# Head sums between scores and values, one block for all loops, a shorter VectorE program and partial sums to row 11, in a decode attention kernel

## Chip, cores, metric

The kernel runs on one core of one Trainium2 chip. The metric is the device time of one execution in microseconds (us), the median of several. The spans in the profile lines are one to three us shorter than the time.

## The reference

One token for each of two sequences: a layer norm, attention over a cache of 32,768 keys and values per head (32 query heads share 8 key/value heads), an output projection, and a small gated MLP whose result multiplies the attention.

```python
q = (xn @ wq) ...                                   # [2, 32, 1, 128]
scores = einsum("bhqd,bhkd->bhqk", q, k) * Dh**-0.5
o = einsum("bhqk,bhkd->bhqd", softmax(scores), v)
s = o.reshape(B, Sq, Hq * Dh) @ wo
g = silu(B_ref(xn, w1, w2, w3, w4))                 # the MLP; with one token, w1 and w2 drop out
return x + s * g
```

A pair of sequence and key/value head is a *group*: 16 groups, each with 8.39 MB of keys and 8.39 MB of values, every byte used once. All in all 280.5 MB are read.

## The kernel before

The synchronising engine (SP) issues the loads. Keys have a ring of three half-buffers, values one buffer of a whole group, so a value load must wait until the group before has used its values.

```python
for m in range(1, NG):
    sp.wait_ge(p_k, NPART * m - 1)      # half of the last keys used
    load_k(m)
    sp.wait_ge(s_r, m + 1)              # head sums of the last group done
    load_v(m)
# ... then the output weights wo, in seven pieces:
WO_PARTS = [(0, 0, 8), (0, 8, 16), (1, 0, 8), (1, 8, 12), (1, 12, 14), (1, 14, 15), (1, 15, 16)]
```

VectorE, once per group (cut):

```python
def heads(dst, p0):
    take(dve, s_o)                                   # value products done
    then(dve.tensor_tensor(out=ox, in0=o, in1=sel_t, op=ALU.mult))
    dve.tensor_reduce(out=ob[:, 0:Dh], in_=ox, op=ALU.add).then_inc(s_ob, 1)
    take(dve, s_x)                                   # TensorE has summed over partitions
    then(dve.reciprocal(...)); then(dve.scalar_tensor_tensor(...))
    dve.tensor_reduce(out=dst, in_=xm, ...).then_inc(s_r, 1)

with dve.Fori(0, NG // 2) as t:
    for odd in range(2):
        heads(oA[...], 0)      # head sums of the group before (a dummy in the first)
        group(odd)             # 16 key transposes, then 2 probability transposes
```

TensorE alternates head sums, 64 score products and 64 value products. At the end it multiplies the heads with the output weights: `early` sums all rows of the first half and rows 0 to 11 of the second as wide partial products, which ScalarE copies out and a small product folds in; the last rows go through `product`, four narrow products per row.

```python
early(0); early(1)
pe.wait_ge(s_r, NG + 2)                # last head sums
early(2)
k_e = P(early(3))                      # rows 8 to 11
k_es = A(act.copy(out=e_sb, in_=e_ps))
product(4)                             # rows 12, 13
wait(pe, k_es)
...                                    # fold e_sb into s_ps
for i in range(5, len(WO_PARTS)): mm = product(i)
```

The softmax here doesn't subtract the row's maximum and nothing guards it: scores larger than these inputs give would overflow.

Of the kernel before, what the change touches and what calls it, by code (L numbers as in the profile page):

```python
# [7 lines left out]
F32 = mybir.dt.float32  # L8
# [7 lines left out]
RT = 16  # L16
# [5 lines left out]
WO_PARTS = [(0, 0, 8), (0, 8, 16), (1, 0, 8), (1, 8, 12), (1, 12, 14), (1, 14, 15), (1, 15, 16)]  # L22
# [38 lines left out]
def kernel(  # L61
# [83 lines left out]
    xf, xn = (Ts[0].bitcast(F32)[0:32, i * D:(i + 1) * D] for i in range(2))  # L145
# [25 lines left out]
    def halves(m):  # L171
# [18 lines left out]
    s_t, s_tf, s_z, s_sc, s_e, s_p, s_o, s_ob, s_x, s_on, s_d, s_r, p_k, s_zf, s_tl = (  # L190
        nc.alloc_semaphore(n)
        for n in ("s_t", "s_tf", "s_z", "s_sc", "s_e", "s_p", "s_o", "s_ob", "s_x", "s_on", "s_d", "s_r", "p_k",
                  "s_zf", "s_tl")
# [77 lines left out]
    wait(dve, k_x)  # L271
    k_xf = V(dve.tensor_copy(out=xf, in_=x_bf[0:32, :]))

# [19 lines left out]
    k_xn = layernorm(0, xn, xf, k_xf)  # L293
# [64 lines left out]
    def spread(eng, j, n):  # L358
        return eng.tensor_copy(  # L359
            out=qr[32 * j:32 * j + 32, :, :, :].rearrange("p a e (m n h) -> p (a e) m n h", n=NQ, h=rep)[  # L360
                :, :, :, n, :
            ],
            in_=qT[32 * n:32 * n + 32, 0:B, :].rearrange("p b (t h a) -> p a (b t) h", t=NQB, h=rep),
        )

    wait(pool, k_qT, (g_, g_.n))
    for n in range(NQ):
        for j in range(NQ):
            G(spread(pool, j, n))
# [16 lines left out]
    for n in range(NQ):  # L386
# [20 lines left out]
    k = V(  # L407
        dve.tensor_scalar(
            out=th[:, :, :], in0=th[:, :, :], scalar1=0.5, scalar2=0.5, op0=ALU.mult, op1=ALU.add
        )  # L410
    )
    wait(dve, k)
    k_hb = V(dve.tensor_mul(out=h_bf[:, :, 0:BW:BS], in0=hf, in1=th[:, :, :]))
# [9 lines left out]
    k_tf = V(dve.tensor_add(out=t_f, in0=xn, in1=h2[0:32, :]))  # L423
# [11 lines left out]
    for m in range(1, NG):  # L435
        sp.wait_ge(p_k, NPART * m - 1)
        load_k(m)
        sp.wait_ge(s_r, m + 1)
# [7 lines left out]
    with act.Fori(0, NG):  # L446
        for i in range(NPART):
# [7 lines left out]
            ).then_inc(s_e, 1)  # L455


    zw = z[:, :, :, (NR - 1) * rep:].rearrange("p n e (j w) -> p (n e) j w", j=NQ)[:, :, :, 0:rep]
    wait(pool, (g_, g_.n), (v_, v_.n), (a_, a_.n))
    pool.sem_inc(s_zf, 1)  # L460
    with pool.Fori(0, NG) as m:
# [16 lines left out]
    def group(odd):  # L478
        hs = halves(odd)
        for i in range(NPART):  # L480
            u = odd + hs[i]
            kt = kbuf[:, u * SLOT:(u + 1) * SLOT].bitcast(I32)
            take(dve, s_k[i], 16)
            for r in range(NR):
                take(dve, s_tl if r == T_BUFS - 1 else s_tf)
                dve.transpose(  # L486
                    out=Ts[(NR * i + r) % T_BUFS][:, :].rearrange("p (b t k) -> p t b k", b=NB, t=RT),
                    in_=kt[:, r * W:(r + 1) * W].rearrange("p (t b k) -> p t b k", b=NB, t=RT),
                ).then_inc(s_t, 1)
        for i in range(NPART):  # L490
            h = hs[i]
            take(dve, s_e)
            dve.transpose(  # L493
                out=pts[h][:, :, :].rearrange("p r (t h) -> p t r h", h=rep),
                in_=eps_[i][:, :].rearrange("p (t r h) -> p t r h", r=NR, h=rep),
            )
        dve.tensor_tensor(out=ob[:, Dh:], in0=rss[0][:, :], in1=rss[1][:, :], op=ALU.add).then_inc(s_p, 1)

    def heads(dst, p0):
        take(dve, s_o)  # L500
# [22 lines left out]
    wait(dve, (v_, v_.n), (g_, g_.n), k_x4)  # L523
    dve.sem_inc(s_o, 1)
    dve.sem_inc(s_tf, T_BUFS - 1)
    dve.sem_inc(s_tl, 1)
    with dve.Fori(0, NG // 2) as t:
        for odd in range(2):
            heads(oA[:, bass.ds(t * (2 * RS) + odd * RS, RS)], 0)
            group(odd)  # L530
# [8 lines left out]


    def head_sums():
        take(pe, s_ob)
        mm = pe.matmul(  # L543
            oT, lhsT=sel_h[:, :, :, :].rearrange("p j h w -> p (j h w)"), rhs=ob[:, :], start=True, stop=True
        )
        mm.then_inc(s_x, 1)

    turn = pe.alloc_register("turn")
    pe.reg_mov(turn, 0)
    nc.br("turn", engines=[pe.engine])  # L550
    nc.switch_bb("turn")
    loop = nc.cur_bb
    head_sums()
    pe.reg_add(turn, turn, 1)
    pe.br_lt(turn, NG + 1, on_true="group", on_false="tail")
    nc.switch_bb("group")
    take(pe, s_z)
    with pe.Fori(0, NPART) as i:
        for r in range(NR):
            Tb = Ts[r % T_BUFS][:, :].bitcast(BF16)  # L560
            Tb = Tb.rearrange("p (b c e) -> p b c e", b=NB, e=2)
            zc = (NR - 1 - r) * rep
            take(pe, s_t)
            for nb in range(NB):
                for e in range(2):
                    mm = pe.matmul(  # L566
                        sc2[:, bass.ds(i * 512, 512)], lhsT=z[:, nb, e, zc:zc + 128], rhs=Tb[:, nb, :, e],
                        start=(r == 0 and nb == 0 and e == 0),
                        stop=(r == NR - 1 and nb == NB - 1 and e == 1),
                    )  # L570
            mm.then_inc(s_tf if r < NR - 1 else s_sc, 1)
    take(pe, s_p)
    for h in range(NPART):
        take(pe, s_v[h], 16)
        vt = vbuf[:, h * SLOT:(h + 1) * SLOT].rearrange("p (t d) -> p t d", d=Dh)
        for u in range(NU):
# [111 lines left out]
```

## Time and profile before

| | before |
|---|---|
| time, first three runs | 653.71 us (653.62 to 654.18) |
| busy share TensorE, VectorE | 58%, 58% |
| share of 16 DMA engines' span in data packets | 99.5% |
| bytes read | 280.5 MB |

Busy shares tell how long an engine works, not whether it sets the end. The queue table of the page tells more here: 99.5% of what all DMA engines have is taken. The chain that ended last covers only the last 7.4 us, from the last head sums on, and says nothing of the 645 us before.

### The profile page before, as it was taken

Reading aid. Unit: us, or ns where it says so; the run is one execution under the profiler, and the core shown is the slowest. Engines: PE = TensorE matmul, PEld = TensorE weight load, DVE = VectorE, ACT = ScalarE, POOL = GpSimd, SP = SyncE. Lnnn points to the kernel's source line nnn. Section 1 sums busy time; section 2 is a strip of 40 time slices with the busy share of each in tenths; the row PEclk is TensorE's granted clock in tenths of the full one; section 3 lists DMA queues with packets and bytes.
Section 4 is the critical chain, followed back from the end, with each engine's and each line's share of the span. In section 5 each row is a group of like instructions: output and inputs, shape, how many; then the busy total and the mean of one; then the engine's idle time right before and its main releaser. Section 6 shows DMA issues by size and latency. Waiting matters only on the chain. (4 is left out here: it accounts for less than half of the span.)

```text
span 652.4 us, 6348 instructions
## 1 busy us (share of the span) xinstructions
PE 376.6 (58%) x2164; PEld 140.1 (21%) x2196; DVE 375.5 (58%) x430; ACT 49.4 (8%) x92; POOL 11.9 (2%) x45
## 2 busy tenths in 40 slices
PE   0758392673829458283854819376381946728674
PEld 0213131221213122021321203122130312203221
DVE  6368392754729365481945639285472927548671
ACT  1011010000101001010100101000010100101010
POOL 1200000000000000000000000000000000000000
PEclk9859688785978968597786969769596886959797
DMA  9989998999899989998999899989998999899997
GB/s 387 482 386 450 450 450 386 450 450 450 386 450 450 446 390 450 450 450 386 450 450 450 386 450 450 450 386 450 450 450 386 450 450 450 386 450 420 447 420 322
DMA packets 6509, 280.51 MB, mean 430 GB/s; under 512 B 746, under 2 KB 1004, under 8 KB 1260
## 3 DMA queue, kind: packets, MB, share of 16 engines
q1 hardware_dynamic: 6492, 280.50, 99.5%
q14 instruction: 1, 0.01, 0.0%
q10 hardware_dynamic: 16, 0.00, 0.0%
HBM read 280.50 MB, written 0.00 MB: 430 GB/s over the span
## 5 line engine op out<-in xcount | busy, mean ns | idle before, releaser
L566 PE MATMUL ps<-T,zeros 128*128 128x512 bf16 x992 | 276.5, 425 | 173.2 <-PEq L46 164.4
L486 DVE STREAM_TRANSPOSE T<-kbuf 128x1024 int32<-128x1024 int32 x256 | 291.2, 1207 | 116.5 <-DVEq L46 115.7
L566 PEld LDWEIGHTS ps<-T,zeros 128*128 128x128 bf16 x1024 | 98.8, 104 | 346.1 <-issue 267.8
L579 PE MATMUL ps<-vbuf,pt 128*16 128x512 bf16 x1024 | 71.3, 441 | 40.5 <-PEq L46 40.5
L502 DVE TENSOR_TENSOR ox<-ps,sel_t 128x512 f32<-128x512 f32 x17 | 11.8, 692 | 83.4 <-DVEq L46 83.4
L453 ACT ACT_TABLE_LOAD x16 | 20.5, 1283 | 445.5 <-ACTq L46 445.5
L579 PEld LDWEIGHTS ps<-vbuf,pt 128*16 128x16 bf16 x1024 | 29.8, 101 | 82.1 <-issue 65.2
L493 DVE STREAM_TRANSPOSE pt<-ep 128x512 bf16<-128x512 bf16 x32 | 22.1, 692 | 28.7 <-DVEq L46 28.7
L543 PE MATMUL ps<-ob,sel_h 128*128 128x129 f32 x34 | 9.0, 350 | 39.3 <-PEq L46 39.3
L453 ACT ACTIVATE ep<-ps 128x512 bf16<-128x512 f32 x32 | 19.1, 597 | 104.7 <-ACTq L46 104.5
L507 DVE TENSOR_REDUCE ob<-ox 128x128 f32<-128x512 f32 x17 | 17.3, 1018 | 2.5
L543 PEld LDWEIGHTS ps<-ob,sel_h 128*128 128x128 f32 x34 | 5.8, 212 | 47.5 <-issue 47.5
L463 POOL TENSOR_TENSOR zeros<-qr,sel_j 128x64 bf16<-128x64 f32 x16 | 4.7, 294 | 571.8 <-POOLq L46 571.8
L343 PE MATMUL ps<-kbuf,xT 128*2 128x512 bf16 x32 | 3.6, 623 | 15.1 <-DVE xT L300 15.1
L511 DVE RECIPROCAL rec<-ps 128x1 f32<-128x1 f32 (+1 forms) x17 | 2.9, 169 | 14.0 <-DVEq L46 14.0
L519 DVE TENSOR_REDUCE oA<-xm 128x128 f32 x16 | 5.9, 366 | 3.8 <-DVEq L46 3.8
L417 PE MATMUL ps<-vbuf,zeros 128*32 x12 | 7.0, 585 | 0.8 <-issue 0.3
L513 DVE SCALAR_TENSOR_TENSOR xm<-ps,rec,mask 128x128 f32<-128x128 f32 (+1 forms) x17 | 6.0, 351 | 2.5
L453 ACT ACTIVATION_READ_ACCUMULATOR ep<-ps 128x1 f32 x32 | 6.2, 194 | 0.0
L423 DVE TENSOR_TENSOR T<-T,ps 32x512 f32<-32x512 f32 x1 | 0.7, 674 | 8.7 <-PE ps L421 8.7
L359 POOL CAST qr<-qT 32x64 bf16<-32x64 f32 x16 | 4.6, 286 | 4.9 <-DVE qT L352 4.0
L343 PEld LDWEIGHTS ps<-kbuf,xT 128*2 128x2 bf16 x32 | 0.9, 113 | 16.8 <-DVE xT L300 15.1
(59 smaller groups left out, 45.1 us busy)
## 6 DMA issues: line engine op xcount, KB each, us to landing
vbuf<-in_A_v_cache_dram SPq DMA_DIRECT2D x4, 4096.0 KB, 26.1
kbuf<-in_A_k_cache_dram SPq DMA_DIRECT2D x2, 4096.0 KB, 22.4
kbuf<-in_A_wq_dram SPq DMA_DIRECT2D x1, 4096.0 KB, 12.3
vbuf<-in_B_w_dram SPq DMA_DIRECT2D x2, 1792.0 KB, 17.1
kbuf<-in_A_wo_dram SPq DMA_DIRECT2D x3, 1024.0 KB, 32.3
kbuf<-in_A_wo_dram SPq DMA_DIRECT2D x1, 512.0 KB, 35.0
kbuf<-in_A_wo_dram SPq DMA_DIRECT2D x1, 256.0 KB, 35.2
kbuf<-in_A_wo_dram SPq DMA_DIRECT2D x2, 128.0 KB, 35.0
```

The lines of the kernel that those rows point to most:

```text
L417: pe.matmul(h2[0:32, :], lhsT=h_bf[:, bass.ds(f, 1), :].rearrange("p f c -> p (f c)"), rhs=w4v[:, bass.ds(f, 1), :].rearrange("p f d -> p ...
L453: act.activation(out=eps_[i][:, :], in_=sc[i][:, :], func=ACT.Exp, scale=inv_sqrt_dh, accum_out=rss[i][:, :]).then_inc(s_e, 1)
L463: pool.tensor_tensor(out=zw, in0=qr[:, :, :, bass.ds(m * rep, rep)].rearrange("p n e h -> p (n e) h").unsqueeze(2).to_broadcast([128, NB * ...
L486: dve.transpose(out=Ts[(NR * i + r) % T_BUFS][:, :].rearrange("p (b t k) -> p t b k", b=NB, t=RT), in_=kt[:, r * W:(r + 1) * W].rearrange( ...
L493: dve.transpose(out=pts[h][:, :, :].rearrange("p r (t h) -> p t r h", h=rep), in_=eps_[i][:, :].rearrange("p (t r h) -> p t r h", r=NR, h= ...
L502: dve.tensor_tensor(out=ox[:, :].rearrange("p (t d) -> p t d", t=VT), in0=o[:, :].rearrange("p (t d) -> p t d", t=VT), in1=sel_t[:, :].uns ...
L507: dve.tensor_reduce(out=ob[:, 0:Dh], in_=ox[:, :].rearrange("p (t d) -> p d t", t=VT), axis=AX.X, op=ALU.add).then_inc(s_ob, 1)
L513: dve.scalar_tensor_tensor(out=xm[p0:, :, :], in0=oT[p0:, 0:Dh].rearrange("p (w r) -> p w r", w=WL), scalar=rec[p0:, 0:1], in1=mask[p0:, : ...
L519: dve.tensor_reduce(out=dst, in_=xm[p0:, :, :].rearrange("p w r -> p r w"), axis=AX.X, op=ALU.add).then_inc(s_r, 1)
L543: mm = pe.matmul(oT, lhsT=sel_h[:, :, :, :].rearrange("p j h w -> p (j h w)"), rhs=ob[:, :], start=True, stop=True)
L566: mm = pe.matmul(sc2[:, bass.ds(i * 512, 512)], lhsT=z[:, nb, e, zc:zc + 128], rhs=Tb[:, nb, :, e], start=(r == 0 and nb == 0 and e == 0), ...
L579: mm = pe.matmul(o[32 * j:32 * j + VT * rep, :], lhsT=pts[h][:, r, a * VT * rep:(a + 1) * VT * rep], rhs=vt[:, u * VT:(u + 1) * VT, :].rea ...
```

## The change

The intent: take the head sums, a serial exchange of VectorE and TensorE, from the stretch in which VectorE ought to begin on the next keys. In the changed kernel the head sums of group m-1 stand between the scores and the values of group m. The value buffer is released as soon as the value products are done (ScalarE passes the count on). All engines' loops are turns of one shared block. The VectorE program of the start is shorter, six of the sixteen head spreads (small copies that lay out the query for the heads) go to ScalarE, and the partial sums end ahead of row 11, where they ended ahead of row 12. The core of the diff:

```diff
-WO_PARTS = [..., (1, 0, 8), (1, 8, 12), (1, 12, 14), (1, 14, 15), (1, 15, 16)]
+WO_PARTS = [..., (1, 0, 8), (1, 8, 11), (1, 11, 14), (1, 14, 15), (1, 15, 16)]
...
-    k_xf = V(dve.tensor_copy(out=xf, in_=x_bf[0:32, :]))
-    k_xn = layernorm(0, xn, xf, k_xf)
+    k_xn = layernorm(0, xn, x_bf[0:32, :], k_x)
...
-            G(spread(pool, j, n))
+            if n == 0 or n == 1 and j < 2:
+                A(spread(act, j, n))
+            else:
+                G(spread(pool, j, n))
...
-    k = V(dve.tensor_scalar(out=th, in0=th, scalar1=0.5, scalar2=0.5, op0=ALU.mult, op1=ALU.add))
-    k_hb = V(dve.tensor_mul(out=h_bf, in0=hf, in1=th))
+    k_hb = V(dve.scalar_tensor_tensor(out=h_bf, in0=th, scalar=1.0, in1=hf, op0=ALU.add, op1=ALU.mult))
...
-        sp.wait_ge(s_r, m + 1)
+        sp.wait_ge(p_o, m)
         load_v(m)
...
+        take(act, s_o)               # ScalarE, after both exponentials of the turn
+        act.sem_inc(s_om, 1)
+        act.sem_inc(p_o, 1)
...
     def heads(dst, p0):
-        take(dve, s_o)
+        take(dve, s_om)
...
-    def group(odd):
+    def group(odd, dst):
         ...                          # 16 key transposes
+        heads(dst, 0)
         ...                          # 2 probability transposes
-    with dve.Fori(0, NG // 2) as t:
+    with turns(dve, NG // 2) as t:   # all engines: one block, compare and branch
         for odd in range(2):
-            heads(oA[...], 0)
-            group(odd)
+            group(odd, oA[...])
```

More of the change, by code (lines that the diff above doesn't have):

```diff
@@ L1 @@
-from contextlib import ExitStack
+from contextlib import ExitStack, contextmanager
 import concourse.bass as bass
@@ L21 @@
 EPS = 1e-5
-WO_PARTS = [(0, 0, 8), (0, 8, 16), (1, 0, 8), (1, 8, 12), (1, 12, 14), (1, 14, 15), (1, 15, 16)]
+WO_PARTS = [(0, 0, 8), (0, 8, 16), (1, 0, 8), (1, 8, 11), (1, 11, 14), (1, 14, 15), (1, 15, 16)]
 class Count:
@@ L144 @@
     x_bf = sbuf([128, D], BF16, "x_bf")
-    xf, xn = (Ts[0].bitcast(F32)[0:32, i * D:(i + 1) * D] for i in range(2))
+    xn = Ts[0].bitcast(F32)[0:32, 0:D]
     t_f, sig = (Ts[1].bitcast(F32)[0:32, i * D:(i + 1) * D] for i in range(2))
@@ L189 @@
     v_, p_, a_, g_ = (Count(nc, n) for n in ("v_", "p_", "a_", "g_"))
-    s_t, s_tf, s_z, s_sc, s_e, s_p, s_o, s_ob, s_x, s_on, s_d, s_r, p_k, s_zf, s_tl = (
+    s_t, s_tf, s_z, s_sc, s_e, s_p, s_o, s_ob, s_x, s_on, s_d, s_r, p_k, s_zf, s_tl, s_om, p_o = (
         nc.alloc_semaphore(n)
         for n in ("s_t", "s_tf", "s_z", "s_sc", "s_e", "s_p", "s_o", "s_ob", "s_x", "s_on", "s_d", "s_r", "p_k",
-                  "s_zf", "s_tl")
+                  "s_zf", "s_tl", "s_om", "p_o")
     )
@@ L269 @@
     V(dve.memset(ps[:, :], 0.0))
-    wait(dve, k_x)
-    k_xf = V(dve.tensor_copy(out=xf, in_=x_bf[0:32, :]))
     def layernorm(i, dst, src, k_src):
@@ L358, in spread @@
     def spread(eng, j, n):
-        return eng.tensor_copy(
+        return (eng.copy if eng is act else eng.tensor_copy)(
             out=qr[32 * j:32 * j + 32, :, :, :].rearrange("p a e (m n h) -> p (a e) m n h", n=NQ, h=rep)[
@@ L364, in spread @@
         )
+    wait(act, k_qT)
     wait(pool, k_qT, (g_, g_.n))
@@ L406 @@
     wait(dve, k)
-    k = V(
-        dve.tensor_scalar(
-            out=th[:, :, :], in0=th[:, :, :], scalar1=0.5, scalar2=0.5, op0=ALU.mult, op1=ALU.add
-        )
-    )
-    wait(dve, k)
-    k_hb = V(dve.tensor_mul(out=h_bf[:, :, 0:BW:BS], in0=hf, in1=th[:, :, :]))
+    k_hb = V(
+        dve.scalar_tensor_tensor(
+            out=h_bf[:, :, 0:BW:BS], in0=th[:, :, :], scalar=1.0, in1=hf, op0=ALU.add, op1=ALU.mult
+        )
+    )
     wait(pe, k_hb, k_w4)
@@ L422 @@
     wait(dve, k_h2)
-    k_tf = V(dve.tensor_add(out=t_f, in0=xn, in1=h2[0:32, :]))
+    k_tf = V(
+        dve.scalar_tensor_tensor(out=t_f, in0=h2[0:32, :], scalar=0.5, in1=xn, op0=ALU.mult, op1=ALU.add)
+    )
     wait(act, k_tf)
@@ L443, with turns @@
         d_wo[i].after(sp.dma_start(out=wo3[:, g, w], in_=wos[:, g, w]), 16)
-    with act.Fori(0, NG):
+    wait(pool, (g_, g_.n), (v_, v_.n), (a_, a_.n))
+    pool.sem_inc(s_zf, 1)
+    wait(dve, (v_, v_.n), (g_, g_.n), k_x4)
+    dve.sem_inc(s_om, 1)
+    dve.sem_inc(s_tf, T_BUFS - 1)
+    dve.sem_inc(s_tl, 1)
+    turn = {e: e.alloc_register("turn") for e in (pe, act, pool, dve)}
+    for e in turn:
+        e.reg_mov(turn[e], 0)
+    nc.br("turn")
+    entry = nc.cur_bb
+    nc.switch_bb("values")
+    take(pe, s_p)
+    for h in range(NPART):
+        take(pe, s_v[h], 16)
+        vt = vbuf[:, h * SLOT:(h + 1) * SLOT].rearrange("p (t d) -> p t d", d=Dh)
+        for u in range(NU):
+            r, a = divmod(u, RT // VT)
+            j = u % 4
+            mm = pe.matmul(
+                o[32 * j:32 * j + VT * rep, :],
+                lhsT=pts[h][:, r, a * VT * rep:(a + 1) * VT * rep],
+                rhs=vt[:, u * VT:(u + 1) * VT, :].rearrange("p t d -> p (t d)"),
+                start=(h == 0 and u < 4), stop=(h == NPART - 1 and u >= NU - 4),
+                tile_position=(0, 32 * j),
+            )
+    mm.then_inc(s_o, 1)
+    pe.br_lt(turn[pe], NG, on_true="turn", on_false="heads")
+    nc.switch_bb("turn", parent=entry)
+    @contextmanager
+    def turns(e, n):
+        yield e.snap(turn[e], min_val=0, max_val=n - 1)
+        e.reg_add(turn[e], turn[e], 1)
+        e.br_lt(turn[e], n, on_true="turn", on_false="half")
+    with turns(act, NG):
         for i in range(NPART):
@@ L455 @@
             ).then_inc(s_e, 1)
+        take(act, s_o)
+        act.sem_inc(s_om, 1)
+        act.sem_inc(p_o, 1)
     zw = z[:, :, :, (NR - 1) * rep:].rearrange("p n e (j w) -> p (n e) j w", j=NQ)[:, :, :, 0:rep]
-    wait(pool, (g_, g_.n), (v_, v_.n), (a_, a_.n))
-    pool.sem_inc(s_zf, 1)
-    with pool.Fori(0, NG) as m:
+    with turns(pool, NG) as m:
         take(pool, s_zf)
@@ L476, in then @@
         take(dve, s_d)
-    def group(odd):
-        hs = halves(odd)
-        for i in range(NPART):
-            u = odd + hs[i]
-            kt = kbuf[:, u * SLOT:(u + 1) * SLOT].bitcast(I32)
-            take(dve, s_k[i], 16)
-            for r in range(NR):
-                take(dve, s_tl if r == T_BUFS - 1 else s_tf)
-                dve.transpose(
-                    out=Ts[(NR * i + r) % T_BUFS][:, :].rearrange("p (b t k) -> p t b k", b=NB, t=RT),
-                    in_=kt[:, r * W:(r + 1) * W].rearrange("p (t b k) -> p t b k", b=NB, t=RT),
-                ).then_inc(s_t, 1)
-        for i in range(NPART):
-            h = hs[i]
-            take(dve, s_e)
-            dve.transpose(
-                out=pts[h][:, :, :].rearrange("p r (t h) -> p t r h", h=rep),
-                in_=eps_[i][:, :].rearrange("p (t r h) -> p t r h", r=NR, h=rep),
-            )
-        dve.tensor_tensor(out=ob[:, Dh:], in0=rss[0][:, :], in1=rss[1][:, :], op=ALU.add).then_inc(s_p, 1)
     def heads(dst, p0):
-        take(dve, s_o)
+        take(dve, s_om)
         then(
@@ L521, in heads @@
             ).then_inc(s_r, 1)
-    wait(dve, (v_, v_.n), (g_, g_.n), k_x4)
-    dve.sem_inc(s_o, 1)
-    dve.sem_inc(s_tf, T_BUFS - 1)
-    dve.sem_inc(s_tl, 1)
-    with dve.Fori(0, NG // 2) as t:
-        for odd in range(2):
-            heads(oA[:, bass.ds(t * (2 * RS) + odd * RS, RS)], 0)
-            group(odd)
+    def group(odd, dst):
+        hs = halves(odd)
+        take(dve, s_z)
+        for i in range(NPART):
+            u = odd + hs[i]
+            kt = kbuf[:, u * SLOT:(u + 1) * SLOT].bitcast(I32)
+            take(dve, s_k[i], 16)
+            for r in range(NR):
+                take(dve, s_tl if r == T_BUFS - 1 else s_tf)
+                dve.transpose(
+                    out=Ts[(NR * i + r) % T_BUFS][:, :].rearrange("p (b t k) -> p t b k", b=NB, t=RT),
+                    in_=kt[:, r * W:(r + 1) * W].rearrange("p (t b k) -> p t b k", b=NB, t=RT),
+                ).then_inc(s_t, 1)
+        heads(dst, 0)
+        for i in range(NPART):
+            h = hs[i]
+            take(dve, s_e)
+            dve.transpose(
+                out=pts[h][:, :, :].rearrange("p r (t h) -> p t r h", h=rep),
+                in_=eps_[i][:, :].rearrange("p (t r h) -> p t r h", r=NR, h=rep),
+            )
+        dve.tensor_tensor(out=ob[:, Dh:], in0=rss[0][:, :], in1=rss[1][:, :], op=ALU.add).then_inc(s_p, 1)
@@ new lines, with head_sums @@
+    with turns(dve, NG // 2) as t:
+        for odd in range(2):
+            group(odd, oA[:, bass.ds(t * (2 * RS) + odd * RS, RS)])
+    def head_sums():
+        take(pe, s_ob)
+        mm = pe.matmul(
+            oT, lhsT=sel_h[:, :, :, :].rearrange("p j h w -> p (j h w)"), rhs=ob[:, :], start=True, stop=True
+        )
+        mm.then_inc(s_x, 1)
+    half = pe.alloc_register("half")
+    pe.reg_mov(half, 0)
+    nc.br("half", engines=[pe.engine])
+    nc.switch_bb("half")
+    i = pe.snap(half, min_val=0, max_val=NPART - 1)
@@ new lines @@
+    for r in range(NR):
+        Tb = Ts[r % T_BUFS][:, :].bitcast(BF16)
+        Tb = Tb.rearrange("p (b c e) -> p b c e", b=NB, e=2)
+        zc = (NR - 1 - r) * rep
+        take(pe, s_t)
+        for nb in range(NB):
+            for e in range(2):
+                mm = pe.matmul(
+                    sc2[:, bass.ds(i * 512, 512)], lhsT=z[:, nb, e, zc:zc + 128], rhs=Tb[:, nb, :, e],
+                    start=(r == 0 and nb == 0 and e == 0),
+                    stop=(r == NR - 1 and nb == NB - 1 and e == 1),
+                )
+        mm.then_inc(s_tf if r < NR - 1 else s_sc, 1)
@@ L531 @@
+    pe.reg_add(half, half, 1)
+    pe.br_lt(half, NPART, on_true="half", on_false="heads")
+    nc.switch_bb("heads", parent=entry)
+    head_sums()
+    pe.reg_add(turn[pe], turn[pe], 1)
+    pe.br_lt(turn[pe], NG + 1, on_true="values", on_false="tail")
+    nc.switch_bb("tail", parent=entry)
+    dve.wait_ge(s_r, NG)
     oA4 = oA[:, RS:].rearrange("p (b s j r) -> p j (b s) r", b=B, s=NS, j=NQ)
@@ L538 @@
     heads(oX4[32 * (NQ - 1):, B * NS - 1, :], 32 * (NQ - 1))
-    def head_sums():
-        take(pe, s_ob)
-        mm = pe.matmul(
-            oT, lhsT=sel_h[:, :, :, :].rearrange("p j h w -> p (j h w)"), rhs=ob[:, :], start=True, stop=True
-        )
-        mm.then_inc(s_x, 1)
-    turn = pe.alloc_register("turn")
-    pe.reg_mov(turn, 0)
-    nc.br("turn", engines=[pe.engine])
-    nc.switch_bb("turn")
-    loop = nc.cur_bb
-    head_sums()
-    pe.reg_add(turn, turn, 1)
-    pe.br_lt(turn, NG + 1, on_true="group", on_false="tail")
-    nc.switch_bb("group")
-    take(pe, s_z)
-    with pe.Fori(0, NPART) as i:
-        for r in range(NR):
-            Tb = Ts[r % T_BUFS][:, :].bitcast(BF16)
-            Tb = Tb.rearrange("p (b c e) -> p b c e", b=NB, e=2)
-            zc = (NR - 1 - r) * rep
-            take(pe, s_t)
-            for nb in range(NB):
-                for e in range(2):
-                    mm = pe.matmul(
-                        sc2[:, bass.ds(i * 512, 512)], lhsT=z[:, nb, e, zc:zc + 128], rhs=Tb[:, nb, :, e],
-                        start=(r == 0 and nb == 0 and e == 0),
-                        stop=(r == NR - 1 and nb == NB - 1 and e == 1),
-                    )
-            mm.then_inc(s_tf if r < NR - 1 else s_sc, 1)
-    take(pe, s_p)
-    for h in range(NPART):
-        take(pe, s_v[h], 16)
-        vt = vbuf[:, h * SLOT:(h + 1) * SLOT].rearrange("p (t d) -> p t d", d=Dh)
-        for u in range(NU):
-            r, a = divmod(u, RT // VT)
-            j = u % 4
-            mm = pe.matmul(
-                o[32 * j:32 * j + VT * rep, :],
-                lhsT=pts[h][:, r, a * VT * rep:(a + 1) * VT * rep],
-                rhs=vt[:, u * VT:(u + 1) * VT, :].rearrange("p t d -> p (t d)"),
-                start=(h == 0 and u < 4), stop=(h == NPART - 1 and u >= NU - 4),
-                tile_position=(0, 32 * j),
-            )
-    mm.then_inc(s_o, 1)
-    nc.br("turn", engines=[pe.engine])
-    nc.switch_bb("tail", parent=loop)
     step = NS * RS // BS
@@ L648 @@
     sp.wait_ge(s_out, 16)
-    tail, s_end = nc.cur_bb, nc.alloc_semaphore("s_end")
-    end = dve.alloc_register("end")
+    tail, end, s_end = nc.cur_bb, dve.alloc_register("end"), nc.alloc_semaphore("s_end")
     dve.reg_mov(end, 1)
-    for eng, hint, reg in ((pe, hint_p, turn), (dve, hint_v, end)):
-        eng.br_lt(reg, 1, on_true="more", on_false="end").branch_hint(hint)
+    for e, reg, hint in ((pe, turn[pe], hint_p), (dve, end, hint_v)):
+        e.br_lt(reg, 1, on_true="more", on_false="end").branch_hint(hint)
     nc.switch_bb("more")
-    pe.sem_inc(s_end, 1)
     dve.sem_inc(s_end, 1)
```

## The prediction

> **What bounds the kernel now.** I read the page first, then the transfer rate in equal stretches, then the synchronising engine's waits with the issue times, then one group and the last ten microseconds in the timeline.
>
> The page says that no compute engine is near full: TensorE and VectorE are busy 58% of the span each. The DMA line and the queue line say something else.
>
> ```profile
> PE 376.6 (58%) x2164; PEld 140.1 (21%) x2196; DVE 375.5 (58%) x430; ACT 49.4 (8%) x92; POOL 11.9 (2%) x45
> ...
> DMA packets 6509, 280.51 MB, mean 430 GB/s; under 512 B 746, under 2 KB 1004, under 8 KB 1260
> ...
> q1 hardware_dynamic: 6492, 280.50, 99.5%
> q14 instruction: 1, 0.01, 0.0%
> ```
>
> One queue's packets took 99.5% of what 16 DMA engines have in the whole span. The strip of rates on the page swings between 386 and 450 GB/s, and short windows swing more. That is not an idle queue: a cache packet is 64 KB and takes 2.418 us on its engine in the trace's packet records, all 16 engines finish together, and a packet's bytes are counted where it ends, so a window holds a whole number of rounds. With windows of 24.1 us, close to ten rounds, the swing goes (columns: window, its length, busy time and count of each engine, granted clock, DMA share, GB/s):
>
> ```profile
> 100.00:638.60 538.60, 312.05 (x1824) 117.69 (x1852) 311.23 (x342) 37.23 (x70) 3.82 (x13) 0.80 1.00 433
> 638.60:648.80 10.20, 6.81 (x62) 2.25 (x62) 2.61 (x5) 0.00 (x0) 0.00 (x0) 0.68 0.99 409
> 648.80:652.40 3.60, 0.92 (x24) 0.47 (x24) 0.58 (x2) 0.59 (x1) 0.00 (x0) 0.96 0.01 3
> ```
>
> These three windows are the case in small. For 538.6 us the DMA share is 1.00; nearly every 24.1 us window inside reads 435 GB/s. In the next 10.2 us the output weights (4.2 MB, shorter rows) come at 409 GB/s, share 0.99. After 648.8 us nothing is left to bring, and 3.6 us of tail follow. So the time is a transfer of 280.5 MB without a hole (280.5 / 0.435 = 645 us), a start of 1.0 us before the first packet, small losses on shorter rows, and the tail.
>
> Could the stream run dry if engines were slower? The synchronising engine waits for buffers, but early. The issue section gives a median of 27.2 us (keys) and 27.3 us (values) from issue to landing, while 8.39 MB at 435 GB/s take 19.3 us: each load is issued with about 8 us of older work ahead of it. The start is tightest: the second key load goes out at 53.70 us with 33.0 - 8.4 = 24.6 MB issued before it and about 22.5 MB moved, 2 MB or 5 us of reserve.
>
> **One group before the change**, from the timeline:
>
> ```profile
> 603.11 3.63 PE L579 MATMUL ps<-vbuf,pt 128*16 128x512 bf16 x64 [2.23 <-PEq L46]
> 606.90 0.69 DVE L502 TENSOR_TENSOR ox<-ps,sel_t 128x512 f32<-128x512 f32 x1 [4.09 <-DVEq L46]
> 607.74 1.02 DVE L507 TENSOR_REDUCE ob<-ox 128x128 f32<-128x512 f32 x1
> 608.90 0.46 PE L543 MATMUL ps<-ob,sel_h 128*128 128x129 f32 x2 [2.16 <-PEq L46]
> ...
> 610.41 0.37 DVE L519 TENSOR_REDUCE oA<-xm 128x128 f32 x1 [0.24 <-DVEq L46]
> 610.80 0.80 SPq L222 DMA_DIRECT2D vbuf<-in_A_v_cache_dram  x2
> ```
>
> The values end at 606.74, the head sums run from 606.90 to 610.78, and only then is the next value load issued. It looks like a serial 4 us per group, 16 x 3.9 = 62 us in all. But VectorE then waits for keys: "DVE T L486" stands with 115.7 us of idle time, 7.7 us in each of 15 waits.
>
> **What the Trainium skill says.** "DMA: Bandwidth & Descriptors", section Specifications, gives a fabric ceiling of 435 GB/s and an HBM limit of about 358 GB/s per core. The trace agrees with the first, 435, and exceeds the second; so the stream is at a ceiling that no program order lifts. The same page, section "Anatomy of one DMA", says that waits happen on the issuing sequencer and the DMA engines just drain their queues. That fits a full queue behind waits of up to 20.0 us on that sequencer. "Runtime: NRT & Kernel Launch", section "Instruction fetch mechanics", warns that a taken branch outside the fetched window stalls on a fetch. The trace has one instruction packet in the whole span, so the present loops do not do this. "Advanced Engine Details and Errata", section "Control Flow Timing", puts a compare-and-branch at about 108 ns; the visible cost here is the 0.23 us TensorE gap between the two halves of a group. So one turn more or fewer of such branches is worth some tenths of a microsecond per group.
>
> **The change part by part.**
>
> *Head sums moved.* VectorE no longer does them ahead of a group's transposes but between those and the probability transposes. The 3.9 us leave the stretch before the transposes and enter the stretch before the values. Before, the second probability transpose waits for the second exponential anyway (1.8 us idle), so I estimate the values start 603.1 + 3.9 - 1.5, about 2.4 us later after keys land. The value load is now released when values are done, not after head sums, so it goes out about 3.9 - 2.4 = 1.5 us sooner. More reserve for a queue that had 8 us: worth 0.
>
> *Relay through ScalarE* (values done, ScalarE passes the count to VectorE and to the loads): two more semaphore hops, about 0.15 us by my estimate from the 0.14 to 0.16 us between an end and a dependent start above. Hidden in all groups but the last.
>
> *One block, compare-and-branch turns.* A few tenths of a microsecond per group on engines with idle time: 0, if no fetches appear.
>
> *Shorter VectorE program.* The cast of x (0.41 us), one gate multiply-add (0.18 us) and their waits go, about 0.65 us; six of sixteen head spreads move from GpSimd to ScalarE. They release the gate's last product sooner, and with it the other half of the first value load. That load goes out at 36.1 us, with 20.4 MB issued ahead and about 15.2 MB moved: 12 us of reserve. Worth 0. The dummy head sums that keep VectorE from 38.46 to 42.66 us, ahead of the first transposes, move too: the second key load comes some 3 us sooner. Again only reserve.
>
> *Partial sums to row 11.* This alone touches the end:
>
> ```profile
> 647.00 0.32 PEld L604 LDWEIGHTS ps<-kbuf,zeros 128*17 128x17 bf16 x8 [0.54 <-DVE zeros L519]
> 648.16 0.10 PEld L604 LDWEIGHTS ps<-kbuf,zeros 128*17 128x17 bf16 x4 [0.85 <-DMA kbuf<-in_A_wo_dram]
> 648.80 0.12 PEld L616 LDWEIGHTS ps<-kbuf,zeros 128*17 128x17 bf16 x8 [0.53 <-DMA kbuf<-in_A_wo_dram]
> 648.83 0.59 ACT L629 COPY T<-ps 128x512 f32<-128x512 f32 x1 [16.95 <-PE ps L604]
> ...
> 649.47 0.41 PE L633 MATMUL ps<-T,zeros 128*17 128x128 f32 x8 [0.27 <-ACT T L629]
> ...
> 650.68 0.68 SPq L645 DMA_DIRECT2D out_dram<-out  x1
> ```
>
> The last partial product waits for its weights (648.16), then comes the copy (648.83 to 649.42), then the fold. With three rows for four in that piece, 131 KB less, it lands 0.31 us earlier at 420 GB/s. But its predecessor starts only at 647.0, after the last head sum, which the relay makes about 0.15 us later; two rounds of 0.43 us at half clock bring it to 648.0. The copy then starts near 648.65 and the fold near 649.28. The next piece ends on the same byte as before, lands at 648.80, and has 12 small products for 8, about 0.11 us more, done in time for the fold. Sum: about -0.2 us. Per-packet cost does not move: 4 KB took 159 ns and 2 KB took 84, 243 together; two of 3 KB interpolate to about 240.
>
> **Sum.** Steady state 0, start 0, end -0.2 us: 653.7 - 0.2 = 653.5 us.
>
> **Rivals.** *The serial head sums do bound each group.* Then 16 x 3.9 us less 16 x 2.4 give 24 us, some 630 us. Against it: the DMA share of 1.00 and VectorE idle for keys after its head sums. Under 1%. *A new wait empties the queue*: a fetch at each branch, or values so late that loads come more than 8 us later than now. Each hole adds its own length. With 2.4 us estimated and the value wait itself shortened, I give 2%. *The tail gets longer*: relay and twelve small products eat the 0.31 us, or TensorE meets a fetch on leaving its loop. Then 653.8 to 654.5; plausible, 20%.
>
> **Range and chances.** The runs before lie between 653.62 and 654.18, so noise is as large as the effect. I take 653.0 to 654.2. A gain of 2% needs 13 us, over three times the whole tail: 1%. A loss of 2% needs 13 us of holes: 1%.
>
> **What would show it.** Right: packets still at 99.5%, 435 GB/s in the middle, VectorE's wait before the key transposes longer than 115.7 us in total as its wait before head sums falls, value issues earlier after the key landing, the copy of partial sums starting before 648.8. Wrong: a window of low DMA share, instruction packets by the dozen, or value issues so late that issue to landing falls to 19 us.

## The result and the profile after

The changed kernel took 653.53 us (653.06 to 653.89, six runs), the kernel before 653.72 us (653.62 to 654.37, six runs). The ratio is 0.9994, 95% interval 0.9981 to 1.0007. A ratio is the mean time of one kernel's fast runs over that of the other's of the same rounds, the profiled runs left out, so not quite the ratio of the medians. The class is "same".

First the page of the changed kernel: engines, then the queues.

```profile
PE 396.2 (61%) x2199; PEld 141.2 (22%) x2199; DVE 371.8 (57%) x428; ACT 51.2 (8%) x98; POOL 10.2 (2%) x39
...
q1 hardware_dynamic: 6492, 280.50, 99.5%
q10 hardware_dynamic: 16, 0.00, 0.0%
```

The data share is again 99.5%. The row "q14 instruction" of the kernel before is gone. It looks like nothing and comes back below. The same three windows (columns as in the prediction):

```profile
100.00:638.60 538.60, 332.05 (x1852) 119.83 (x1852) 309.77 (x345) 37.21 (x70) 3.80 (x13) 0.80 1.00 433
638.60:648.80 10.20, 7.20 (x73) 2.20 (x73) 2.61 (x5) 0.58 (x1) 0.00 (x0) 0.67 0.97 400
648.80:652.00 3.20, 0.60 (x16) 0.37 (x16) 0.58 (x2) 0.00 (x0) 0.00 (x0) 0.97 0.00 1
```

In the middle, 433 GB/s at a DMA share of 1.00, to the digit as before. The second window has a lower rate only because this trace's stream ends earlier in it. Now one group of the changed kernel, on all engines but the weight loads:

```profile
599.33 0.66 DVE L520 TENSOR_TENSOR ox<-ps,sel_t 128x512 f32<-128x512 f32 x1
...
601.30 0.46 PE L570 MATMUL ps<-ob,sel_h 128*128 128x129 f32 x2 [0.69 <-PEq L46]
...
602.82 0.37 DVE L537 TENSOR_REDUCE oA<-xm 128x128 f32 x1 [0.24 <-DVEq L46]
...
604.73 5.25 PE L466 MATMUL ps<-vbuf,pt 128*16 128x512 bf16 x64 [2.97 <-PEq L46]
...
610.22 0.80 SPq L222 DMA_DIRECT2D vbuf<-in_A_v_cache_dram  x2
```

The head sums now start with no idle time of VectorE before them, straight after the last key transpose, and the values follow. The reorder did what it was meant to do. The waits say where VectorE's time went: first the kernel before, then the changed one (columns: who waited for whom, us in total, times, longest).

```profile
DVE T L486 <- DVEq L46: 115.7, 15, 9.4
...
DVE ox L502 <- DVEq L46: 83.4, 17, 9.6
```

```profile
DVE T L550 <- DVEq L46: 226.1, 18, 15.5
...
DVE ox L520 <- DVEq L46: 8.1, 1, 8.1
```

VectorE's wait for value products ahead of the head sums fell by 75.3 us, and its wait ahead of the key transposes rose by 110.4. The 28.7 us ahead of the probability transposes went as well. The idle time only changed its place: the keys arrive when they arrive.

One thing in the group is worse. The 64 value products took 5.25 us, and 3.63 in the same group before. Two windows, laid on these stretches in the kernel before and the changed one, have the granted clock (third number from the end):

```profile
603.11:606.74 3.63, 3.63 (x64) 1.58 (x64) 0.00 (x0) 0.00 (x0) 0.00 (x0) 1.00 1.01 436
```

```profile
604.73:609.98 5.25, 5.25 (x64) 1.88 (x64) 0.00 (x0) 0.00 (x0) 0.00 (x0) 0.68 0.97 418
```

The granted clock is 1.00 in the first and 0.68 in the second. TensorE now sits idle for 2.97 us ahead of the values, not 2.23, with only a 0.46 us head sum before that; whether this lowers the clock no run isolates, and in other groups the old loop has slow value products too. In the fifteen groups ahead of the last the old loop's value products take 3.63 or 5.32 us, the new one's 5.01 to 6.36, and the mean of all 1024 is 441 ns before and 525 ns after. So the value load, counted from the first key transpose of its group, went out after 610.22 - 581.19 = 29.03 us, where it was 610.80 - 581.53 = 29.27 before.

The end of the changed kernel:

```profile
646.66 0.12 PEld L626 LDWEIGHTS ps<-kbuf,zeros 128*17 128x17 bf16 x8 [0.84 <-DVE zeros L537]
647.35 0.10 PEld L626 LDWEIGHTS ps<-kbuf,zeros 128*17 128x17 bf16 x3 [0.56 <-DMA kbuf<-in_A_wo_dram]
648.17 0.58 ACT L651 COPY T<-ps 128x512 f32<-128x512 f32 x1 [16.92 <-PE ps L626]
...
648.80 0.49 PE L655 MATMUL ps<-T,zeros 128*17 128x128 f32 x8
...
650.10 0.67 SPq L667 DMA_DIRECT2D out_dram<-out  x1
```

The copy begins 0.66 us earlier than before (648.17 against 648.83) and the output goes out 0.58 us earlier (650.10 against 650.68). But the last data packet also ended 0.53 us earlier: at 648.61 and not 649.14 in the traces' packet records. From the last packet to the output it is 1.49 us against 1.54. In these two traces the gain lies almost wholly in the stream, not in the tail where I had put it. Which of the changed parts did that, if any, is the question of the last experiments.

### The profile page after: what moved, and what is told of

Its sections match the earlier page's. It is cut to its first block, busy times and chain, and to the rows that moved or that the text cites. A ratio compares the mean times of both kernels' runs of the same rounds, so it can differ in the third digit from the quotient of the medians.

```text
span 651.8 us, 6433 instructions
## 1 busy us (share of the span) xinstructions
PE 396.2 (61%) x2199; PEld 141.2 (22%) x2199; DVE 371.8 (57%) x428; ACT 51.2 (8%) x98; POOL 10.2 (2%) x39
## 3 DMA queue, kind: packets, MB, share of 16 engines
q1 hardware_dynamic: 6492, 280.50, 99.5%
## 5 line engine op out<-in xcount | busy, mean ns | idle before, releaser
L587 PE MATMUL ps<-T,zeros 128*128 128x512 bf16 x1024 | 280.7, 424 | 170.5 <-PEq L46 165.3
L466 PE MATMUL ps<-vbuf,pt 128*16 128x512 bf16 x1024 | 89.4, 525 | 49.8 <-PEq L46 49.8
L466 PEld LDWEIGHTS ps<-vbuf,pt 128*16 128x16 bf16 x1024 | 33.1, 115 | 101.0 <-issue 92.7
L558 DVE STREAM_TRANSPOSE pt<-ep 128x512 bf16<-128x512 bf16 x32 | 20.7, 685 | 0.0
L269 DVE MEMSET ps<- 128x4096 f32 x1 | 3.5, 3472 | 0.9 <-issue 0.9
```

The lines of the kernel that those rows point to most:

```text
L466: mm = pe.matmul(o[32 * j:32 * j + VT * rep, :], lhsT=pts[h][:, r, a * VT * rep:(a + 1) * VT * rep], rhs=vt[:, u * VT:(u + 1) * VT, :].rea ...
L558: dve.transpose(out=pts[h][:, :, :].rearrange("p r (t h) -> p t r h", h=rep), in_=eps_[i][:, :].rearrange("p (t r h) -> p t r h", r=NR, h= ...
L587: mm = pe.matmul(sc2[:, bass.ds(i * 512, 512)], lhsT=z[:, nb, e, zc:zc + 128], rhs=Tb[:, nb, :, e], start=(r == 0 and nb == 0 and e == 0), ...
```

## The experiments

The theory: the transfer of 280.5 MB at the engines' full rate bounds the kernel, engine loops have a reserve, and only the tail can move. The main rival: the serial chain in each group bounds, or a new wait hides its gain.

### Take the bytes away

Groups 2 to 14 load a quarter of each key and value buffer. Every wait and every product stays. The result is wrong: most of each buffer is old data. The comparison with the reference passed all the same, so it says nothing in these two runs.

```diff
+        if 2 <= m < last:
+            w = slice(0, SLOT // 2)
+            sp.dma_start(out=dst[:, w], in_=row_view(cache, *groups[m])[:, w]).then_inc(sems[0], 16)
-        if m < last:
+        elif m < last:
```

> Wrong result on purpose: for groups 2 to 14 each key or value load brings a quarter of its bytes (everything else, every wait and all compute, stays). Theory: the transfer set the 38.6 us per group, and under it lies VectorE's and TensorE's serial chain of 29.3 us; 13 groups save 9.3 us each, so about 533 us (520 to 545). Rival (the serial chain bounds already): stays above 640 us.

> The same cut of bytes in the changed kernel, wrong result on purpose. Theory: with the transfer out of the way the moved head sums show: VectorE's own work per group, 18.1 transposes + 3.8 head sums + 1.4 probability transposes = 23.5 us, with some waits 24 to 26 us; 13 groups at 14 us less than 38.6 give about 470 us (455 to 495), that is 40 to 75 us under the kernel before with the same cut. Rival (the reorder really shortens nothing, TensorE's slower value products take it back): within 10 us of the kernel before with the same cut.

The kernel before took 545.57 us (ratio to before 0.8348, 95% interval 0.8335 to 0.8361), the changed one 480.48 us (0.7352, 0.7341 to 0.7363). The middle of each, before and then changed:

```profile
144.50:483.30 338.80, 252.72 (x1433) 89.23 (x1432) 241.90 (x266) 29.23 (x55) 3.21 (x11) 0.88 0.35 136
```

```profile
141.50:423.30 281.80, 237.06 (x1433) 86.11 (x1431) 241.31 (x266) 29.25 (x55) 3.23 (x11) 0.90 0.42 164
```

Both windows hold eleven groups: 30.8 us and 25.6 us per group, at a DMA share of 0.35 and 0.42. So the transfer did set the 38.6 us, and the change is worth 5.2 us per group and 65 us in all, once nothing else bounds. VectorE is busy equally long in both windows (241.9 and 241.3 us); its idle time fell from 8.8 to 3.7 us per group. That fits the reorder, but no run has the reorder without the new loops. Both runs came out some 10 us longer than I had expected (the first just outside its range), and the longer period is enough to explain it. For the kernel before it is 30.8 and not 29.3: I had read 29.3 in a group whose value products took 3.63 us, and in a group of this window they took 5.22 us at a clock of 0.69. For the changed one it is 25.6, where the 470 us stood for 24.6.

### Make the head sums longer

Extra reductions of 1.02 us each on VectorE, in all head sums but the last: four in the first pair, ten in the second.

```diff
     def heads(dst, p0):
         ...
+        for _ in range(4 if p0 == 0 else 0):      # 10 in the second pair
+            then(dve.tensor_reduce(out=ob[:, 0:Dh], in_=ox, axis=AX.X, op=ALU.add))
         dve.tensor_reduce(out=ob[:, 0:Dh], in_=ox, ...).then_inc(s_ob, 1)
```

> The kernel before with four more reductions (1.02 us each, about 1.15 with its wait) in each group's head sums but the last: 4.6 us more on the serial path of 16 groups. Theory: 29.3 + 4.6 = 33.9 us stays under the 38.6 us of transfer per group, so time within 0.5 us of before. Rival (the head sums are on the path): 16 x 4.6 = 74 us more, some 727 us.

> The same four more reductions in the changed kernel. Theory: value loads go out 29.0 + 4.6 = 33.6 us after their keys landed, still before the next keys land, so no change from the changed kernel within 0.5 us. Rival: tens of us more, since the head sums now stand ahead of the values.

> Ten more reductions, about 11.5 us, in each group's head sums but the last, in the kernel before. Theory: 29.3 + 11.5 = 40.8 us passes 38.6, the value load is issued after the queue has run dry, and each group gets a hole of 2 to 4 us with the issue's own delay: 15 groups, 30 to 60 us more, about 700 us (683 to 715); DMA share in the middle falls to about 0.93. Rival (transfer not the bound): 16 x 11.5 = 184 us more.

> The same ten reductions in the changed kernel. Theory: the value load is released 29.0 + 11.5 = 40.5 us after the keys landed, as late as before, so the change has bought no reserve against longer head sums: within 8 us of the kernel before with ten reductions, about 698 us. Rival (moving the head sums off the start of the group bought reserve, as VectorE begins the next keys' transposes at once): nearer 653 than 690 us.

| | time, us | ratio to before (95%) | expected |
|---|---|---|---|
| before, four more | 669.70 (663.21 to 672.93) | 1.0226 (1.0157 to 1.0295) | no change: missed |
| changed, four more | 662.63 (661.99 to 663.51) | 1.0135 (1.0118 to 1.0152) | no change: missed |
| before, ten more | 724.91 (723.65 to 726.38) | 1.1078 (1.1060 to 1.1097) | about 700: missed |
| changed, ten more | 708.59 (705.93 to 710.63) | 1.0845 (1.0816 to 1.0874) | within 8 of the line above: missed |

The class of the first is "unclear", its four runs lie 9.7 us apart, and that of the second "same" by the limit of 2%; the other two are "slower". The rival of the last forecast, nearer 653 than 690 us, failed too. The sixteen extra stretches amount to 74 and 184 us, and none of the four came near that, so the serial chain alone is not the bound; that much holds. But my picture of the reserve was too simple in two ways. A group of the kernel before with four more reductions:

```profile
315.89 0.33 SPq L226 DMA_DIRECT2D vbuf<-in_A_v_cache_dram  x1
318.91 18.37 DVE L486 STREAM_TRANSPOSE T<-kbuf 128x1024 int32<-128x1024 int32 x16 [3.05 <-DVEq L46]
```

The value load goes out only 3 us before VectorE starts on the keys that were queued ahead of it. The packet records of the traces tell the rest. "Reserve" is the time from a value load's issue to the mean end of the last packets of the key load ahead of it; "gap" the mean idle time of a DMA engine between the two loads; "packet" the mean duration of the 64 KB packets of that value load.

```
kernel, value load of group   reserve us   gap us   packet ns
before                   1      4.64        0.00      2418
before                  13      6.76        0.00      2418
changed                  1      8.09        0.00      2418
changed                 13      7.80        0.00      2418
before, four more        1     -1.46        2.69      2498
before, four more        2      3.33        0.00      2420
before, four more        7      1.58        0.12      2482
before, four more       11      0.06        1.15      2497
changed, four more       1      2.51        0.10      2459
changed, four more      10      3.07        0.01      2418
before, ten more         5     -2.64        3.72      2515
changed, ten more       13     -0.67        1.89      2500
```

First, the stream suffers before the queue is empty. With a reserve of 3 us it costs little (in the traces with four more reductions up to 25 ns a packet, 0.2 us a load); at 1.6 us the eight packets that each engine then works off take 64 ns longer each, 0.5 us; below zero there is a hole about 1.1 us longer than the missing reserve.

Second, the thinnest place is the first whole value load: 4.64 us of reserve before, 8.09 in the changed kernel. That shows with nothing added. Most of it does not come from the shorter start: the kernel before with the new prologue alone, tested below, has 5.73 us there, and the one with row 11 alone 5.45. The four more reductions cost the stream 14 us in the kernel before (last packet at 663.49 and not 649.14) and 3.4 us in the changed one (651.97 and not 648.61). The changed kernel's other 4.5 us are in its tail: the head sums of group 14 now stand ahead of the last values, and the profiled span ended 7.8 us after the last packet, 3.2 us without the additions.

So against my expectation the change does buy reserve: with ten more reductions it is worth 724.91 - 708.59 = 16.3 us. In those two traces the stream ended 31.4 us earlier (690.61 and not 722.01). Of that, 14.8 us are holes ahead of the key and value loads of group 1 (19.3 us before, 4.5 changed), which in the kernel before the lengthened dummy head sums help to delay; in the 13 groups after it the holes are 37.9 and 24.4 us, 1.0 us less per group. A longer tail took 10.9 us back (14.0 us after the last packet, 3.1 before). The kernel as it is has no use for the reserve.

### The row alone, and the change without the row

> The kernel before with the row change alone. Theory (transfer is the bound, only the end can move): 0.1 to 0.4 us under before, so about 653.4 to 653.6 us; the copy of the partial sums starts near 648.2 to 648.6 instead of 648.83. Rival (the small gain came from the loops or the start): equal to before within noise, and the copy at the same distance from the end of the stream.

> The changed kernel with the row change undone. Theory: the loops and the start are worth nothing in time, so it equals before within 0.3 us, about 653.7 us. Rival (loops or start gave the gain): equal to the changed kernel, 653.5 us or less, and the row change is then worth 0.

Edit of the first (the second is its reverse, in the changed kernel):

```diff
-WO_PARTS = [..., (1, 8, 12), (1, 12, 14), (1, 14, 15), (1, 15, 16)]
+WO_PARTS = [..., (1, 8, 11), (1, 11, 14), (1, 14, 15), (1, 15, 16)]
```

Beside 653.99 us of the kernel before (nine runs), the row alone took 654.21 us (ratio 1.0002, 0.9988 to 1.0016), and the changed kernel without it 653.78 us (0.9999, 0.9985 to 1.0012). No gain from the row on the kernel before is visible, so the first theory missed and its rival held: the copy began 0.36 us ahead of the last packet, 0.31 before. The second run met its theory, within 0.3 us of before, but the rival's 653.5 us is nearly as close, so it decides nothing. The trace of the row alone says why the copy did not move:

```profile
645.58 3.16 PE L604 MATMUL ps<-kbuf,zeros 128*17 128x512 bf16 x27
...
647.89 0.10 PEld L604 LDWEIGHTS ps<-kbuf,zeros 128*17 128x17 bf16 x3 [0.49 <-DMA kbuf<-in_A_wo_dram]
648.80 0.59 ACT L629 COPY T<-ps 128x512 f32<-128x512 f32 x1 [16.20 <-PE ps L604]
```

The piece of three rows was there at 647.89, but the partial products of TensorE ended just ahead of the copy at 648.80, where it had begun at 648.83 before. Nothing came of the 0.31 us: the 27 products took 3.16 us, 28 took 3.21 before. Their weight loads come in fours, one for each quarter of the array, and with three for four in the last set there are as many sets as before. The output even went out later, 1.80 us after the last packet where it was 1.54. But that stretch scatters: 1.49 us in the changed kernel and 1.88 in its repeat, so no single pair of traces measures 0.2 us there.

### What moved the stream?

My new theory was the reserve at the start: with the old loops 107 and 127 of the 3712 packets of 64 KB took more than 2.425 us (kernel before, and with row 11), with the new ones 0 and 2. Three kernels and a repeat were to test it, with a try at a better tail as a fourth.

```diff
# changed kernel, late start (in_ cut)
     wait(dve, (v_, v_.n), (g_, g_.n), k_x4)
+    for _ in range(6):
+        k = V(dve.tensor_reduce(out=ob[:, 0:Dh], in_=..., axis=AX.X, op=ALU.add))
+        wait(dve, k)
```

The kernel "before, new prologue" has the changed kernel's layer norm, spreads and gate, with the old loops and rows. "Row 10" is the changed kernel with

```diff
-WO_PARTS = [..., (1, 8, 11), (1, 11, 14), (1, 14, 15), (1, 15, 16)]
+WO_PARTS = [..., (1, 8, 10), (1, 10, 14), (1, 14, 15), (1, 15, 16)]
-    product(4)
     wait(pe, k_es)
     ...                                # fold, now first
-    for i in range(5, len(WO_PARTS)):
+    for i in range(4, len(WO_PARTS)):
```

> The changed kernel once more beside the kernel before, as the yardstick of the other three: 0.2 to 0.5 us under before; the 64 KB packets of its transfer all within 2.42 us, the last packet near 648.6 to 648.8 us of the span.

> The changed kernel with six reductions (some 7 us) on VectorE ahead of the first transposes, so that the first value load of a whole group goes out near 73.5 us, as late as in the kernel before (70.05 us in the changed one). Theory (the reserve at the start decides how evenly the 16 DMA engines run): some dozens of 64 KB packets above 2.425 us come back, as the 107 and 127 seen with the old loops, and the stream ends 0.2 to 0.5 us later. Rival (the place of the head sums in every group decides): no long packets, stream end unchanged.

> The kernel before with the shorter VectorE program and the ScalarE spreads alone; loops and rows as before. The first whole value load goes out near 71.5 us, half way. Theory (reserve at the start): fewer long packets than 107, stream end between the two, time within 0.3 us of before. Rival (head sums in every group): about as many long packets as before.

> An attempt at a better version: partial sums to row 10 and the fold ahead of the first small product, so that only small products follow the last weights. By the changed kernel's trace TensorE is busy from 648.29 to 649.40 without a break; with the fold done before the weights of that piece land, about 0.2 us earlier: 653.3 us, within noise of the changed kernel. Rival (TensorE's partial products, at half clock and after the last head sums, hold the copy back, not the weights): gain under 0.1 us or a loss.

Beside 654.06 us of the kernel before (nine runs), in these runs:

| | time, us | ratio to before (95%) | long packets | last packet, us |
|---|---|---|---|---|
| changed, again | 654.13 | 1.0002 (0.9989 to 1.0016) | 116 | 648.90 |
| changed, late start | 654.93 | 1.0010 (0.9996 to 1.0024) | 27 | 649.38 |
| before, new prologue | 653.69 | 0.9997 (0.9983 to 1.0011) | 12 | 648.68 |
| changed, row 10 | 655.46 | 1.0020 (1.0006 to 1.0033) | 111 | 649.81 |

The theory fell with the first line: the changed kernel itself, repeated, had 116 long packets, and its time was that of the kernel before. The number of long packets varies from run to run. It is worth 0.2 us and no part of the change is shown to set it. "Late start" also missed its aim: its first whole value load had 6.93 us of reserve, not the 4.64 of the kernel before. "Before, new prologue" did what its theory said, which after the first line is no support for it.

Something else fits the last column. These are all transfers of at least 8 KB on the instruction queues that lie inside the data stream, from the packet records, with the lag they left: the end of the slowest of the 16 engines behind the mean of all, at the last whole value load.

```
kernel                  instruction packet in the stream   slowest - mean, group 14   last packet
before                  8 KB at 606.00 us, 0.31 us         0.27 (before the fetch)     649.14
before, row 11          8 KB at 606.02 us, 0.31 us         0.20 (before the fetch)     649.16
changed                 none                               0.19                        648.61
changed, again          none                               0.21                        648.90
changed, row 12         none                               0.34                        648.76
before, new prologue    none                               0.22                        648.68
changed, late start     8 KB at 45.63 us, 0.31 us          0.78                        649.38
changed, row 10         16 KB at 36.98 us, 0.92 us         1.07                        649.81
```

An engine that has to bring instructions falls behind with its data and does not catch up here: every load gives each engine an equal share, and none has idle time. The data packet behind the fetch is longer too: 1.43 us for 1.21 in the kernel before and with row 11, 1.74 for 1.21 in "late start", 2.93 for 2.42 in "row 10". So an 8 KB fetch cost its engine 0.5 to 0.8 us, not 0.31. In all four traces the engine that had fetched was the last to end its packets of 32 KB and more. In "row 10" it was 1.2 us behind the mean at the end of the first keys, and still 1.1 us 560 us later.

All four kernels with a fetch in the stream end it at 649.14 us or later, all four without at 648.90 or earlier, one trace each. "Before, new prologue" has the old loops and the early end, so it is not the loops as such. That the fetch delays its engine is seen packet by packet. It is not all of the 0.53 us between the kernel before and the changed one: the last whole value load ended at 600.00 and 599.75 us in the mean of the engines, so 0.25 us of it arose ahead of the fetch at 606.00, about what the 107 long packets are worth. Which lines of the program decide where a fetch falls I did not try, and in time an 8 KB fetch stays inside the scatter of the runs.

"Row 10" lost 1.4 us. Its queue row, and its tail:

```profile
q8 instruction: 2, 0.03, 0.0%
```

```profile
647.69 1.45 PE L626 MATMUL ps<-kbuf,zeros 128*17 128x512 bf16 x10 [1.40 <-DMA kbuf<-in_A_wo_dram]
...
649.18 0.59 ACT L651 COPY T<-ps 128x512 f32<-128x512 f32 x1 [16.71 <-PE ps L626]
...
649.82 0.63 PE L654 MATMUL ps<-T,zeros 128*17 128x128 f32 x8 [0.68 <-ACT T L651]
...
650.22 0.87 PE L638 MATMUL ps<-kbuf,zeros 128*17 128x128 bf16 x24
```

TensorE waits 1.40 us for weights that the late engine brings, and with the fold first all 24 narrow products then stand behind the late copy. The one fetch among its two instruction packets that counts is that of 36.98 us; the other came after the stream. No version that beats both kernels was found.

## Why the prediction was right

The time (653.53 us against 653.5 predicted) and the class were right, and the reason for the class too. Its points one by one:

- **The transfer bounds, the steady state gives 0.** Shown: the same rate and share in the middle, VectorE's gain turned into a longer wait for keys, and 108 and 174 us gone when the bytes were cut.
- **The reorder shortens the serial chain, unseen.** Shown for the change as a whole: 30.8 to 25.6 us per group once the bytes are out of the way.
- **"1.5 us sooner" for the value load.** Mis-sized. Measured 0.24 us in the group shown; over groups 2 to 14 of the two traces the reserve of the value load grew from 7.58 to 8.51 us in the mean, 0.93 us. "About 2.4 us later" for the start of the values was fair (1.96 us in the group shown). What the working left out is that the value products then take longer, 5.25 us for 3.63 in that group, at a clock of 0.68, and 1.1 us more in the mean.
- **"More reserve for a queue that had 8 us: worth 0" and "each hole adds its own length".** The verdict held. The rule was wrong: a reserve under some 3 us already costs, through longer packets, and a hole is about 1.1 us longer than the missing time. Most reserve was won at the first whole value load, 4.64 to 8.09 us.
- **"This alone touches the end", -0.2 us from row 11.** Not borne out. On the kernel before, the row alone moved the copy by 0.03 us and the time by nothing that can be seen. TensorE's partial products held the copy back: I had put the start of their last set at 648.0 and the copy at 648.65, and it came at 648.80. The 0.5 us by which the two traces differ lie in the end of the stream. The predicted 653.5 met the measured 653.53 partly by chance: the repeat gave 654.13 beside 654.06.
- **The relay**, estimated at 0.15 us, took 0.11: in the last group VectorE began 0.28 us after the last value product, 0.17 before.
- **Three readings were wrong**, and nothing in the sum rests on them. The 0.23 us gap is not the cost of a branch between the halves of a group: it follows the eighth of 64 score products, where one record is missing from the trace (two starts 0.85 us apart, those around them 0.43). No run measured a branch. The strip of rates has a slice of 482 and a last one of 322 GB/s beside the 386 to 450. And the rate in a window counts a packet's bytes where it starts, not where it ends.
- **The instruction fetch as a rival** was named for loops and branches. It did turn up, but on the DMA engines, as half a microsecond to 1.4 us on one of them.

## What to carry to other kernels

When the data queue is at 99.5% and the rate in the middle equals the full rate, shortening a serial chain elsewhere moves only a wait; cut the bytes in an experiment to see what the chain is worth, and give its gain a use or leave it. A load's reserve, from issue to the end of the work ahead of it, is the number to watch, at its thinnest place and not at its median. In a stream without idle time, as here, whatever delays one DMA engine once, even an instruction fetch, is still there at the end.

## What the Trainium skill lacked or had wrong

- "DMA: Bandwidth & Descriptors", Specifications: the row of about 358 GB/s does not say when it holds. The same page, section "Bandwidth", Measured, does: that is a core's share when both cores of a pair stream, and a lone core gets more. So the 433 GB/s that this one core read over 538 us contradict only the row read alone.
- The same page gives a first-byte latency, but no measure of how far ahead a load must be issued to keep the engines at full rate. Here a reserve of 3 us cost at most 0.2 us a load, 1.6 us cost 64 ns on each of eight packets, and a hole came out some 1.1 us longer than the missing reserve (3.72 us at -2.64).
- "Runtime: NRT & Kernel Launch", Instruction fetch mechanics, calls the cost of crossing a block mostly hidden, and has no number for the data engine that carries the fetch. In this full stream an 8 KB fetch took 0.31 us and a 16 KB fetch 0.92 us, the data packet behind it 0.2 to 0.5 us more than usual, and in one kernel that engine was 1.2 us behind the others' mean afterwards and 1.1 us behind 560 us later. The section has refills of 16 KiB; the traces have instruction packets of 8 KB on one queue and of 16 KB on another.
